# Direct preparation of the first weight jobs, on-chip shifted copies, another tile order in the first pair of blocks, and a zero-product start on TensorE

## The chip, the cores and the metric

The kernel runs on one core of a Trainium2 chip. The metric is the device time of one execution in microseconds (us), lower is better. The engines are named as the profile names them: PE is the matrix engine TensorE, PEld its weight loads, DVE the vector engine, ACT the scalar engine, POOL is GpSimd, SP the sync engine, which here does nothing but issue transfers (DMAs); SPq is its queue.

## What is computed

```python
# attention-like part: causal convolution, 7 taps per head, taps softmaxed
w = exp(weight - max(weight)); w = w / (sum(w) + 1e-9)
out[b, s, h, :] = sum over k of w[h, k] * x_pad[b, s + k, h, :]     # x: 2 x 4096 x 192
x = out.reshape(8192, 192)
# first layer
x = (sigmoid(x @ w_gate) * (x @ w_val)) @ w_out                     # 192 -> 1536 -> 192
# second layer
h = x @ w_in
g = where(h > 0, h, exp(min(h, 0)) - 1)
out = g @ w_out2                                                    # 192 -> 2048 -> 192
```

The activations are float32, the five weight matrices of the two layers are float64.

## The kernel before

**Tiling.** The 8192 tokens are 16 blocks of `TB` = 512. Blocks are taken in `GROUPS`: 0 to 2, 3 to 5, then pairs. Within a group, first all tiles of the first layer (kind 1, 12 tiles of 128 hidden units per block), then those of the second (kind 2, 16 tiles, two to a step). The list `steps` holds them; in the first group blocks 0 and 1 are interleaved tile by tile (`todo[:2]`), and block 2 follows alone. So steps 0 to 23 are kind 1 of blocks 0 and 1, steps 24 to 35 kind 1 of block 2, and step 36 begins kind 2 of blocks 0 and 1.

**Precision.** Each float32 factor is held as a high and a low part (float32r), and three products high x high, low x high and high x low are summed. 192 rows are 128 + 64; the matmuls work on 64 rows each, in pairs on the two halves of the array (`HALVES`). An activation block therefore has three parts: `n` (first 128 rows), `s` (the same with its halves exchanged, made by the DMAs of `exchange`, L144) and `r` (last 64 rows, doubled by the DMAs at L196).

**A step.** `front` (L280) makes the hidden tile of a step: 18 matmuls, 9 pairs, into two banks of the pool `ps_w`, which has four. `ew1` (L294) is ACT's sigmoid (L297) and DVE's product `g` (L299); that product frees the banks. For kind 2 `ew2` (L302) runs relu and exp on ACT (L309, L310) and `g` on DVE (L313), for each of the two banks. `split_hi` (ACT, L320) and `split_lo` (DVE, L326) make `gh` and `gl`, and `back` (L329) multiplies them with the output weights, `LAG` = 2 steps later; for two interleaved blocks one `back` takes both, 20 matmuls per tile. Since a front needs two of four banks, front k + 2 cannot finish its first products before the `g` of step k.

**Weights.** 34 jobs, `prep_in` (L252) and `prep_out` (L259), turn float64 into high and low float32r. `fetch` (L203) reads the tile from DRAM twice: `s` as it is, `m` shifted by two bytes, so that the bits below the high part lie in one 32-bit word. Then `narrow` (L219) runs ACT's absolute value (L232) and five DVE passes over 128x384 (L234, L236, L240, L242, L245), and `low` (L249) is a sixth. A job's parts are pieces of a generator; the table `PREPARED` says how many pieces are done by which step, and `CONV` says at which step the pieces of a block's convolution run. Both are due times written by hand: the program is recorded in that order, and each engine runs its instructions strictly in order.

**The start.** L447 to L460: transfers of the taps, x and the first three jobs are issued on SP; POOL makes an identity, ACT scales it by the taps (L131), and PE convolves the r part of blocks 0 and 1 and the n part of block 1 with these diagonals (L169, 14 float32 products, each two PE instructions); DVE convolves the n part of block 0 (L178, L176). L185 and L188 split the results.

**The change of layer.** At steps 36 and 37 the results of block 2's first layer are copied out of the accumulators by `sums` (L355: `one`, `two`). `early` (L514) lets `ew2` put these two copies between the two halves of a step.

Of the kernel before, what the change touches and what calls it, by code (L numbers as in the profile page):

```python
# [8 lines left out]
F32 = mybir.dt.float32  # L9
# [17 lines left out]
LAG = 2  # L27

# [7 lines left out]
    (-13.5, 0), (-11.5, 6), (-10.5, 9), (-9.5, 9), (-8, 12), (-7, 17), (-5.5, 17), (-1, 20), (21.5, 118),  # L36
# [5 lines left out]
    (0, 1): [-19, -10.5, -10, -10],  # L42
    (1, 0): [-18, -6.5, -6],
    (2, 0): [8.5 + k for k in range(7)] + [16.5, 17.5],
    (2, 1): [2.5 + k for k in range(6)] + [14.5, 18.5, 19.5, 20.5, 53.5, 54.5, 55.5],
# [11 lines left out]
def conv_glu_elu_kernel(  # L57
# [81 lines left out]
    def parts(kind, b, c):  # L139
        t = [xsp.tile([P, TB], F32R, tag=f"{c}{x}", name=f"x{c}{x}") for x in "hl"]  # L140
        parts_t.setdefault((kind, b), {})[c] = t
        return t

    def exchange(kind, b):  # L144

        for t, n in zip(parts(kind, b, "s"), parts_t[kind, b]["n"]):
            nc.sync.dma_start(f32(t[DR:]), f32(n[0:DR]))  # L147
            nc.sync.dma_start(f32(t[0:DR]), f32(n[DR:]))  # L148

    def load_x(b, i):  # L150
# [5 lines left out]
        else:  # L156
            for h in range(2):
                bi, t0 = divmod((b + h) * TB, S)
                nc.sync.dma_start(t[DR * h:DR * (h + 1)], xp[P:D, bi, t0:t0 + TB + PAD])
        yield  # L160

    def conv(b, i):
# [18 lines left out]
        for blocks in ([0], [1]) if i and b == 2 else ([0, 1], ) if i else ([0], ):  # L181
# [10 lines left out]
            if i:  # L192
                for n, ts, r in zip(blocks, made, rows):
                    other = slice(DR * (1 - n), DR * (2 - n))
                    for t in ts:
                        nc.sync.dma_start(f32(t[other]), f32(t[r]))  # L196
# [6 lines left out]
    def fetch(s, src, shift):  # L203

        n = P * 4 - shift
        src, s = src.bitcast(I16), s.bitcast(I16)
        if len(src.shape) == 3:
            m = D * 4 - shift
            d = s.rearrange("p (k m) -> p k m", k=src.shape[0])
            nc.sync.dma_start(d[:, :, 0:m], src.rearrange("k p m -> p k m")[:, :, shift:shift + m])  # L210
            return

        for i in range(2):
            d = s[DR * i:DR * (i + 1), 0:P * 8].rearrange("p (c m) -> p c m", c=2)
            e = src[:, P * 4 * i:P * 4 * (i + 1)].rearrange("(c p) m -> p c m", c=2)
            nc.sync.dma_start(d[:, :, 0:n], e[:, :, shift:shift + n])  # L216
        nc.sync.dma_start(s[:, P * 8:P * 8 + n], src[:, P * 8 + shift:P * 8 + shift + n])  # L217

    def narrow(src):  # L219
# [356 lines left out]
```

## Time and profile before

| | us |
|---|---|
| median of 3 runs | 1242.89 |
| lowest and highest run | 1242.01, 1244.04 |
| the profiled execution, its own time | 1242.56 |
| its span, first to last instruction | 1240.7 |
| what lies around the span | 1.86 |

Of the span PE is busy for 98%, PEld for 87%, DVE for 70%, ACT for 64%. The profile cuts the span in 40 slices: PE is at nine tenths or more in all but the first and the last, while DVE is at eight or nine tenths in slices 2 to 7 (31 to 217 us) and at five to eight afterwards. The DMA engines are busiest in the first six slices. A row of the timeline gives start, duration, engine, line, operation, out<-in, and in square brackets the idle time before it and what ended that. The "busy" of a matmul is modelled and overlaps its neighbours, so that pace is read from the starts.

### The profile page before, as it was taken

What the parts mean: (1) busy time and instruction counts of PE and PEld (TensorE: products, weight loads), DVE (VectorE), ACT (ScalarE), POOL (GpSimd) and SP (SyncE); (2) the same over time, 40 slices, a digit from 0 to 9 for tenths busy, and PEclk for the clock granted to TensorE, in tenths of its full rate; (3) what the DMA queues carried; (4) which work ended last, traced back from release to release, by engine and by line L of the source; (5) the groups of instructions that cost most, each with busy time, mean ns of one, the idle gap of its engine ahead of it and who ended that gap; (6) DMA issues with size and microseconds to landing.
All of it is one profiled execution on the core that took longest, in us unless ns stands there. A gap on an engine that the chain in (4) does not pass through costs nothing.

```text
span 1240.7 us, 25326 instructions
## 1 busy us (share of the span) xinstructions
PE 1215.8 (98%) x10268; PEld 1085.1 (87%) x10268; DVE 864.5 (70%) x1370; ACT 792.4 (64%) x1406; POOL 79.7 (6%) x63
## 2 busy tenths in 40 slices
PE   5999999999999999999999999999999999999997
PEld 2888789888889999999999889997888889998785
DVE  6898899785457876477665776666766667665564
ACT  4455688864348886348854498545884468744785
POOL 0000010100011000011000010010100100001100
PEclk9999999999999999999999999999999999999999
DMA  7756541311011020111111111020110211111100
GB/s 202 203 165 186 155 123 40 86 41 41 15 27 44 18 60 14 31 35 43 32 31 34 28 44 38 23 60 2 43 44 27 52 25 26 37 36 27 26 18 18
DMA packets 48965, 68.28 MB, mean 55 GB/s; under 512 B 6864, under 2 KB 29392, under 8 KB 48848
## 3 DMA queue, kind: packets, MB, share of 16 engines
q1 hardware_dynamic: 48848, 66.67, 20.4%
q8 instruction: 80, 1.31, 0.5%
q14 instruction: 37, 0.30, 0.1%
HBM read 33.09 MB, written 6.29 MB: 32 GB/s over the span
## 4 chain that ended last, share of the span: by engine, by line
PE 89%; DVE 3%; DMA 3%; SPq 2%; ACT 2%; issue 1%; DVEq 0%; ACTq 0%
PE ps L278 49%; PE a L278 40%; DMA s<-in_w_dram 2%; SPq L216 1%; DVE gl L326 1%; DVE g L299 1%; DMA m<-in_w_dram 0%; DVE xcv L176 0%; DVE r L245 0%; ACT e L310 0%; ACT e L309 0%; SPq L217 0%; ACT t L232 0%; SPq L148 0%; SPq L147 0%
## 5 line engine op out<-in xcount | busy, mean ns | idle before, releaser
L320 ACT CAST gh<-g 128x512 fp32r<-128x512 f32 x448 | 272.8, 618 | 181.5 <-DVE g L299 141.4
L326 DVE TENSOR_TENSOR gl<-g,gh 128x512 fp32r<-128x512 f32 x448 | 336.0, 764 | 75.3 <-ACT gh L320 64.7
L278 PE MATMUL a<-gh,w4s 64*128 64x512 f32 x1536 | 295.7, 392 | 0.1
L313 DVE SCALAR_TENSOR_TENSOR g<-e,ps 128x512 f32<-128x512 f32 x256 | 174.2, 686 | 117.9 <-ACT e L310 116.0
L278 PE MATMUL a<-gh,w2s 64*128 64x512 f32 x1152 | 251.8, 391 | 0.0
L278 PE MATMUL a<-gl,w4s 64*128 64x512 f32 x1024 | 244.2, 392 | 0.4 <-DVE gl L326 0.4
L299 DVE TENSOR_TENSOR g<-e,ps 128x512 f32<-128x512 f32 x192 | 131.5, 685 | 151.9 <-ACT e L297 146.8
L297 ACT ACTIVATE e<-ps 128x512 f32<-128x512 f32 x192 | 114.5, 596 | 179.1 <-PE ps L278 178.1
L278 PEld LDWEIGHTS a<-gh,w4s 64*128 64x128 f32 x1536 | 197.4, 185 | 17.0 <-DVE one L367 1.5
L278 PE MATMUL a<-gl,w2s 64*128 64x512 f32 x768 | 205.1, 392 | 1.5 <-DVE gl L326 1.5
L278 PEld LDWEIGHTS a<-gh,w2s 64*128 64x128 f32 x1152 | 163.0, 185 | 14.8 <-ACT gh L320 0.3
L309 ACT ACTIVATE e<-ps 128x512 f32<-128x512 f32 x256 | 150.5, 588 | 28.6 <-PE ps L278 28.0
L310 ACT ACTIVATE e<-e 128x512 f32<-128x512 f32 x256 | 161.9, 633 | 8.1
L278 PE MATMUL ps<-xsh,w1h 64*128 64x512 f32 x384 | 151.8, 395 | 5.6 <-DMA xsh<-xnh 5.3
L278 PEld LDWEIGHTS a<-gl,w4s 64*128 64x128 f32 x1024 | 145.1, 184 | 10.4 <-DVE gl L326 0.8
L278 PE MATMUL ps<-xsh,w1l 64*128 64x512 f32 x384 | 151.2, 394 | 0.0
L278 PE MATMUL ps<-xsl,w1h 64*128 64x512 f32 x384 | 150.6, 392 | 0.0
L278 PE MATMUL ps<-xnh,w1l 64*128 64x512 f32 x384 | 145.0, 393 | 0.0
L278 PE MATMUL ps<-xnh,w1h 64*128 64x512 f32 x384 | 144.7, 392 | 0.0
L278 PE MATMUL ps<-xnl,w1h 64*128 64x512 f32 x384 | 144.4, 392 | 0.0
L278 PEld LDWEIGHTS a<-gl,w2s 64*128 64x128 f32 x768 | 114.6, 184 | 12.7 <-DVE gl L326 3.3
L278 PE MATMUL ps<-xrh,w1h 64*128 64x512 f32 x384 | 120.2, 393 | 2.1 <-DMA xrh<-xrh 2.1
(92 smaller groups left out, 2565.2 us busy)
## 6 DMA issues: line engine op xcount, KB each, us to landing
xsh<-xnh SPq DMA_DIRECT2D x64, 128.0 KB, 2.3
xsl<-xnl SPq DMA_DIRECT2D x64, 128.0 KB, 2.3
s<-in_w_dram SPq DMA_DIRECT2D x60, 128.0 KB, 3.1
m<-in_w_dram SPq DMA_DIRECT2D x60, 127.8 KB, 3.0
three<-two SPq DMA_DIRECT2D x48, 128.0 KB, 2.2
s<-in_w_dram SPq DMA_DIRECT2D x14, 384.0 KB, 3.4
m<-in_w_dram SPq DMA_DIRECT2D x14, 383.5 KB, 3.9
x<-in_xp_dram SPq DMA_DIRECT2D x16, 259.0 KB, 3.2
```

The costliest lines, as they stand in the source:

```text
L216: nc.sync.dma_start(d[:, :, 0:n], e[:, :, shift:shift + n])
L278: return nc.tensor.matmul(ps, w, x, start=first, stop=last)
L297: nc.scalar.activation(s, gate, AF.Sigmoid)
L299: nc.vector.tensor_mul(g, s, val)
L309: nc.scalar.activation(e, h, AF.Relu, scale=-1.0)
L310: nc.scalar.activation(e, e, AF.Exp, scale=-1.0)
L313: nc.vector.scalar_tensor_tensor(g, e, -1.0, h, ALU.add, ALU.max)
L320: nc.scalar.copy(gh, g)
L326: nc.vector.tensor_sub(gl, g, f32(gh))
```

## The change

1. **Weights.** `m` is no longer read from DRAM. The first six jobs (`DIRECT`) have no `m`: their fifth pass takes nine bits of the high word and 15 of the low one, in two DVE instructions instead of one (24 bits instead of 25). The other 28 jobs make `m` by a DMA from `s` on the chip. `s` has four buffers instead of three, `m` two; jobs are fetched four ahead.
2. **Parts of x.** High and low parts lie in one tile, so that `exchange` is two DMAs instead of four, and the doubling of `r` one instead of two.
3. **Order of a front.** Both halves take part `n` first, then `s`, then `r`; the weights' chunk is chosen by `n ^ i`. Before, one half began with `n` and the other with `s`.
4. **Order of the steps.** Blocks 0 and 1 begin 0, 0, 1, 1 and go on 0, 1, 0, 1; the first back stands behind the fifth front.
5. **Start.** The two transfers of block 0's r part are issued on ACT's queue. PE begins with three float32 products of a tile of zeros.
6. **Change of layer.** The copies of block 2 no longer stand between the halves of a step, and the back of step 34 stands before the front of step 37.
7. `PREPARED` and `CONV` have other due times: 14 pieces before the first step instead of 20; block 2's convolution four steps later.

```diff
@@
-    (-13.5, 0), (-11.5, 6), (-10.5, 9), (-9.5, 9), (-8, 12), (-7, 17), (-5.5, 17), (-1, 20), (21.5, 118),
+    (-14.5, 0), (-13.5, 3), (-12, 3), (-11.5, 6), (-10, 6), (-8, 12), (-6.5, 12), (-1, 14), (18.5, 101), (21.5, 114),
...
-    (2, 0): [8.5 + k for k in range(7)] + [16.5, 17.5],
+    (2, 0): [12.5 + k for k in range(7)] + [20.5, 21.5],
...
     def exchange(kind, b):
-        for t, n in zip(parts(kind, b, "s"), parts_t[kind, b]["n"]):
-            nc.sync.dma_start(f32(t[DR:]), f32(n[0:DR]))
-            nc.sync.dma_start(f32(t[0:DR]), f32(n[DR:]))
+        parts(kind, b, "s")
+        n, s = (f32(parts_t[kind, b][c]) for c in "ns")
+        nc.sync.dma_start(s[DR:], n[0:DR])
+        nc.sync.dma_start(s[0:DR], n[DR:])
...
-                nc.sync.dma_start(t[DR * h:DR * (h + 1)], xp[P:D, bi, t0:t0 + TB + PAD])
+                (nc.sync if b else nc.scalar).dma_start(t[DR * h:DR * (h + 1)], xp[P:D, bi, t0:t0 + TB + PAD])
...
-    def narrow(src):
+    def narrow(src, copied):
...
-        s = stage.tile([P, n], I64, tag="s", name="s", bufs=3)
-        m = stage.tile([P, n], I64, tag="m", name="m", bufs=3)
-        fetch(s, src, 0)
-        fetch(m, src, 1)
...
+        s = stage.tile([P, n], I64, tag="s", name="s", bufs=4)
+        fetch(s, src)
+        words = s.bitcast(I32).rearrange("p (n two) -> p n two", two=2)
+        high = words[:, :, 1]
+        yield
+        if copied:
+            m = stage.tile([P, n], I64, tag="m", name="m", bufs=2)
+            nc.sync.dma_start(m.bitcast(I16)[:, 0:4 * n - 1], s.bitcast(I16)[:, 1:])
...
-        nc.vector.tensor_scalar(r, mid, 0x1FFFFFF, None, ALU.bitwise_and)
...
+        if copied:
+            nc.vector.tensor_scalar(r, mid, 0x1FFFFFF, None, ALU.bitwise_and)
+        else:
+            nc.vector.tensor_scalar(r, high, 0x1FF, 15, ALU.bitwise_and, ALU.logical_shift_left)
+            nc.vector.scalar_tensor_tensor(r, words[:, :, 0], 17, r, ALU.logical_shift_right, ALU.bitwise_or)
...
-        held = [[x[c] for c in "nsr"], [x[c] for c in "snr"]]
-        for c in range(3):
-            for k in range(3):
+        for n, part in enumerate("nsr"):
+            xh, xl = x[part][:, 0], x[part][:, 1]
+            for k, (wt, xt) in enumerate(((h, xh), (l, xh), (h, xl))):
                 for i, rows in enumerate(HALVES):
-                    xh, xl = held[i][c]
-                    wt, xt = ((h, xh), (l, xh), (h, xl))[k]
-                    mm(ps[i], wt[rows, c], xt[rows], c + k == 0, c + k == 4)
+                    mm(ps[i], wt[rows, n ^ i if n < 2 else n], xt[rows], n + k == 0, n + k == 4)
...
+                turns = [x for pair in zip(*todo[:2]) for x in pair]
+                if kind == 1:
+                    turns[1:3] = turns[2:0:-1]
+                todo[:2] = [turns]
...
+        warm = ew.tile([P, TB], F32, tag="g", name="warm", bufs=4)
+        nc.vector.memset(warm, 0.0)
+        ps = ps_w.tile([P, TB], F32, tag="w", name="ps")
+        for k in range(3):
+            nc.tensor.matmul(ps, warm[:, 0:P], warm, start=True, stop=True)
...
-            early = [end for k, _, end in ends if now and k < kind]
+            early = [end for k, _, end in ends if now and now[1] > 1 and k < kind]
```

The program's order on the engines shows what this moves. First PE from the start of the program, before; the numbers tell tiles apart: `ps_278` and `ps_279` are the two banks of step 0, block 0's parts are `xnh_186` and `xsh_196`, block 1's `xnh_254` and `xsh_258`.

```order
L169 MATMUL ps_162<-x1_102,gh_140 128x512 x4
L169 MATMUL ps_162<-x1_102,gl_141 128x512 x3
L169 MATMUL ps_171<-x0_113,gh_150 128x512 x4
L169 MATMUL ps_171<-x0_113,gl_151 128x512 x3
L278 MATMUL ps_278<-xnh_186,w1h_85 128x512
L278 MATMUL ps_279<-xsh_196,w1h_85 128x512
...
L278 MATMUL ps_278<-xrl_217,w1h_85 128x512
L278 MATMUL ps_279<-xrl_217,w1h_85 128x512
L278 MATMUL ps_319<-xnh_254,w1h_85 128x512
L278 MATMUL ps_320<-xsh_258,w1h_85 128x512
```

The same place in the changed program, where block 0's parts are `xn_191`, `xs_194` and `xr_203`:

```order
L466 MATMUL ps_122<-warm_120 128x512 x3
L171 MATMUL ps_160<-x1_102,gh_138 128x512 x4
L171 MATMUL ps_160<-x1_102,gl_139 128x512 x3
L171 MATMUL ps_169<-x0_109,gh_148 128x512 x4
L171 MATMUL ps_169<-x0_109,gl_149 128x512 x3
L280 MATMUL ps_242<-xn_191,w1h_85 128x512
L280 MATMUL ps_243<-xn_191,w1h_85 128x512
...
L280 MATMUL ps_242<-xs_194,w1h_85 128x512
L280 MATMUL ps_243<-xs_194,w1h_85 128x512
...
L280 MATMUL ps_280<-xn_191,w1h_85 128x512
L280 MATMUL ps_281<-xn_191,w1h_85 128x512
```

The zero products stand first, a front begins with six matmuls that need no exchanged part, and the second front is block 0's again. Second place, DVE from the end of block 0's convolution through the first weight job, before (`t_183`, `h_190`, `r_202` belong to that job):

```order
L176 SCALAR_TENSOR_TENSOR xcv_159<-x0_100,cwn_95,xcv_159 128x512 x6
L234 TENSOR_SCALAR t_183<-t_183 128x384
L236 TENSOR_SCALAR t_183<-t_183 128x384
L240 SCALAR_TENSOR_TENSOR h_190<-s_105,t_183 128x384
L242 TENSOR_SCALAR t_183<-h_190 128x384
L188 TENSOR_TENSOR xnl_187<-xcv_159,xnh_186 128x512
L245 TENSOR_SCALAR r_202<-m_106 128x384
L250 SCALAR_TENSOR_TENSOR w1l_86<-r_202,t_183 128x384
```

and in the changed program (`t_180`, `h_187`, `r_198`):

```order
L178 SCALAR_TENSOR_TENSOR xcv_157<-x0_100,cwn_95,xcv_157 128x512 x5
L231 TENSOR_SCALAR t_180<-t_180 128x384
L178 SCALAR_TENSOR_TENSOR xcv_157<-x0_100,cwn_95,xcv_157 128x512
L233 TENSOR_SCALAR t_180<-t_180 128x384
L237 SCALAR_TENSOR_TENSOR h_187<-s_105,t_180 128x384
L190 TENSOR_TENSOR xn_191<-xcv_157,xn_191 128x512
L239 TENSOR_SCALAR t_180<-h_187 128x384
L245 TENSOR_SCALAR r_198<-s_105 128x384
L246 SCALAR_TENSOR_TENSOR r_198<-s_105,r_198 128x384
L251 SCALAR_TENSOR_TENSOR w1l_86<-r_198,t_180 128x384
L190 TENSOR_TENSOR xr_203<-ps_160,xr_203 64x512
```

The first pass of the job now stands before the convolution's last tap, and L246 is the added pass. Third place, ACT at steps 36 and 37, before (`ps_2182` and `ps_2183` are the banks of step 37):

```order
L309 ACTIVATE e_2235<-ps_2182 128x512
L310 ACTIVATE e_2235<-e_2235 128x512
L366 COPY one_2240<-a2_1673 128x512
L366 COPY two_2241<-a3_1674 128x512
L309 ACTIVATE e_2246<-ps_2183 128x512
L310 ACTIVATE e_2246<-e_2246 128x512
```

and in the changed program (`ps_2128` and `ps_2129` are step 37's):

```order
L309 ACTIVATE e_2173<-ps_2128 128x512
L310 ACTIVATE e_2173<-e_2173 128x512
L309 ACTIVATE e_2178<-ps_2129 128x512
L310 ACTIVATE e_2178<-e_2178 128x512
L366 COPY one_2183<-a2_1612 128x512
L366 COPY two_2184<-a3_1613 128x512
```

The two copies moved behind the second half.

## Rows read from the trace of the kernel before

**Rows 1.** The page, part 1: busy time, share of the span, instructions.
```profile
PE 1215.8 (98%) x10268; PEld 1085.1 (87%) x10268; DVE 864.5 (70%) x1370; ACT 792.4 (64%) x1406; POOL 79.7 (6%) x63
```

**Rows 2.** Stretches: length, busy time (instructions), granted clock, DMA share, GB/s; PE, last DVE.
```profile
20.00:25.00 5.00, 2.53 (x19) 1.00 0.70 191
25.00:30.00 5.00, 0.01 (x2) 0.63 0.73 208
30.00:35.00 5.00, 5.00 (x30) 0.69 0.96 276
155.00:160.00 5.00, 3.45 (x27) 0.94 0.07 16
160.00:165.00 5.00, 5.00 (x35) 0.71 0.63 145
400.00:800.00 400.00, 400.00 (x3433) 1.00 0.14 34
...
40.00:100.00 60.00, 58.89 (x129) 1.00 0.59 174
```

**Rows 3.** Timeline of PE from 5 to 45 us.
```profile
5.55 5.51 PE L169 MATMUL ps<-x,gh 128*128 128x512 f32 x8 [5.55 <-DMA x<-in_xp_dram]
10.89 2.74 PE L169 MATMUL ps<-x,gl 128*128 128x512 f32 x6
19.57 0.49 PE L278 MATMUL ps<-xnh,w1h 64*128 64x512 f32 x1
23.58 0.50 PE L278 MATMUL ps<-xrh,w1h 64*128 64x512 f32 x1 [2.12 <-DMA xrh<-xrh]
29.98 0.76 PE L278 MATMUL ps<-xsh,w1h 64*128 64x512 f32 x1 [5.33 <-DMA xsh<-xnh]
44.48 0.76 PE L278 MATMUL a<-gh,w2s 64*128 64x512 f32 x4
```

**Rows 4.** Timeline of ACT and SP to 28 us; last a row of DMA issues.
```profile
9.65 0.54 ACT L232 ACTIVATE t<-s 128x384 f32<-128x384 f32 x1
20.96 0.50 SPq L196 DMA_DIRECT2D xrh<-xrh  x1
27.49 0.50 SPq L147 DMA_DIRECT2D xsh<-xnh  x1
...
m<-in_w_dram SPq DMA_DIRECT2D x3, 383.5 KB, 5.6
```

**Rows 5.** Timeline of DVE: a low part of a job, and one whole step.
```profile
12.87 0.56 DVE L250 SCALAR_TENSOR_TENSOR w1l<-r,t 128x384 fp32r<-128x384 int32 x1
...
61.02 0.68 DVE L326 TENSOR_TENSOR gl<-g,gh 128x512 fp32r<-128x512 f32 x1
61.62 0.68 DVE L299 TENSOR_TENSOR g<-e,ps 128x512 f32<-128x512 f32 x1
62.22 0.35 DVE L234 TENSOR_SCALAR t<-t 128x384 f32<-128x384 f32 x1
62.49 0.74 DVE L176 SCALAR_TENSOR_TENSOR xcv<-x,cwn,xcv 128x512 f32<-128x512 f32 x1
63.15 0.35 DVE L236 TENSOR_SCALAR t<-t 128x384 int32<-128x384 int32 x1
63.53 0.56 DVE L240 SCALAR_TENSOR_TENSOR h<-s,t 128x384 int32<-128x384 int32 x1
64.13 0.36 DVE L242 TENSOR_SCALAR t<-h 128x384 int32<-128x384 int32 x1
64.40 0.68 DVE L326 TENSOR_TENSOR gl<-g,gh 128x512 fp32r<-128x512 f32 x1
```

**Rows 6.** Timeline of PE and ACT where the layers change.
```profile
159.35 0.74 PE L278 MATMUL ps<-xsh,w3h 64*128 64x512 f32 x1 [1.55 <-DVE g L313]
162.87 0.85 PE L278 MATMUL a<-gh,w4s 64*128 64x512 f32 x4
...
156.36 0.57 ACT L366 COPY one<-a 128x512 f32<-128x512 f32 x1
157.30 0.61 ACT L309 ACTIVATE e<-ps 128x512 f32<-128x512 f32 x1
```

More of the change, by code (lines that the diff above doesn't have):

```diff
@@ L192, in conv, with fetch @@
             if i:
[L193 to L196, printed above, removed]
+                for n, r in zip(blocks, rows):
+                    t = f32(parts_t[1, b + n]["r"])
+                    nc.sync.dma_start(t[DR * (1 - n):DR * (2 - n)], t[r])
                 yield
-    def fetch(s, src, shift):
-        n = P * 4 - shift
-        src, s = src.bitcast(I16), s.bitcast(I16)
+    def fetch(s, src):
@@ L217, in fetch @@
-        nc.sync.dma_start(s[:, P * 8:P * 8 + n], src[:, P * 8 + shift:P * 8 + shift + n])
-    def narrow(src):
-        n = 3 * P
-        s = stage.tile([P, n], I64, tag="s", name="s", bufs=3)
-        m = stage.tile([P, n], I64, tag="m", name="m", bufs=3)
-        fetch(s, src, 0)
-        fetch(m, src, 1)
-        high = s.bitcast(I32).rearrange("p (n two) -> p n two", two=2)[:, :, 1]
-        mid = m.bitcast(I32).rearrange("p (n two) -> p n two", two=2)[:, :, 0]
+        for i, rows in enumerate(HALVES):
+            d = s[rows, 0:2 * P].rearrange("p (c m) -> p c m", c=2)
+            nc.sync.dma_start(d, src[:, P * i:P * (i + 1)].rearrange("(c p) m -> p c m", c=2))
@@ L265, in prep_out @@
             nc.scalar.copy(d[:, :, c, m], h[:, :, k])
[L266 removed]
+            low(d[:, :, o, q], r[:, :, k], unit, t[:, :, k])
             yield
@@ L443, in weights @@
                     yield n
-                if n + 3 < len(jobs):
-                    next(jobs[n + 3])
+                if n + 4 < len(jobs):
+                    next(jobs[n + 4])
         nc.sync.dma_start(cws, cw)
@@ L490, in conv_glu_elu_kernel @@
             now = steps[i] if 0 <= i < len(steps) else None
-            past = [i - LAG]
-            if now and now[1] < 2:
-                past = [i - LAG - 1, i - LAG] if now[1] else []
-            elif i >= LAG and i - LAG < len(steps) and steps[i - LAG][1] < 2:
-                past = [i - LAG - 1, i - LAG] if steps[i - LAG][1] else []
-            past = [steps[k] + (held.pop(k), ) for k in past if 0 <= k < len(steps)]
-            if past and past[0][1] == 0:
-                past = [past]
-            else:
-                past = [[x] for x in past]
+            past = [steps[k] for k in [i - LAG] if 0 <= k < len(steps)]
+            if past and past[0][1] < 2:
+                kind, b, j = past[0]
+                past = [(kind, n, j) for n in range(2)] if b else []
             if now:
@@ L505, in conv_glu_elu_kernel @@
             ends = []
-            for turns in past:
-                k, _, j, _ = turns[0]
-                ends += back(k, range(j, j + k), [(b, gs) for _, b, _, gs in turns])
+            if past:
+                kind_k, _, j_k = past[0]
+                ends = back(kind_k, range(j_k, j_k + kind_k), [(x[1], held.pop(index[x])) for x in past])
             his = split_hi(held.get(i - 1, []))
```

49 lines of the change are left out of this document (23 added, 26 removed).

## The prediction

> **What bounds the kernel now.** I read the page first, then stretches, then the timeline where the stretches are odd. PE is busy for 98% of the span [rows 1], so that time can only come from its gaps and its slow stretches. In 400 to 800 us it does 3433 matmuls without a gap [rows 2]: 0.1165 us each, 0.233 us a pair, so a front of 9 pairs takes 2.1 us and a back of two tiles (10 pairs) 2.33 us. The first 45 us are different: 2.53 us of work in 20 to 25, nothing in 25 to 30, then a granted clock of 0.69, a mean of the levels 1.2 and 2.4 GHz [rows 2]. The timeline says why [rows 3]. Step 0 starts at 19.57 when the convolutions end; at 23.58 it has waited 2.12 us for the doubled `r`, whose DMA SP issued only at 20.96 because weight transfers stood before it [rows 4]; step 1 belongs to block 1, and its first pair needs the exchanged part, issued at 27.49 [rows 4], so PE stands 5.33 us until 29.98 [rows 3] and comes back at half clock. The sixth front ends at 44.48, where a back begins [rows 3]. The second limit is DVE, 58.89 of 60 us in 40 to 100 [rows 2]. The second gap lies where the layers change: PE waits until 159.35 for a `g` of DVE and then runs one front in 3.52 us, to 162.87 [rows 6], at a clock of 0.71 [rows 2].
>
> **Part A, the start.** All edits at the start go together, because one chain results.
>
> PE. A float32 product is two PE passes. In the first row eight passes take 5.51 us; later six take 2.74, at starts 0.43 apart [rows 3]: the clock's two levels. 28 passes at the upper one are 12.0 us, and from 5.55 to 19.57 they took 14.0: the slow beginning cost 2.0 us. The zeros are six passes. PE can begin when DVE has filled a 128x512 tile; no row has this, so I bound it by an idle engine's start and DVE's 128x512 passes (0.74 us at most [rows 5]), which gives 0.8 to 1.6, and take 1.4. The zeros end at 4.0 if all are fast and at 6.5 if all are slow; if they take over just the 2.0 us that the convolutions lost, at 1.4 + 6 x 0.43 + 2.0 = 6.0, later than x arrives. I take that; the convolutions end at 6.0 + 12.0 = 18.0 instead of 19.57. Behind them, in order, stands step 0, whose `s` and `r` are no longer behind `m`: 1.2 MB of `m` for three jobs leave the queue before them, so I give it no wait.
>
> The x transfers on ACT's queue put two issues before ACT's other work: 0.5 to 0.6 us each by SP's rows [rows 4], of which I take 0.4 us as delay after overlap with the wait for the taps. ACT's first pass of job 0, done at 10.2 before [rows 4], is then done at 10.6. The Trainium skill, DMA: Bandwidth & Descriptors, section Issuing engines are not separate DMA queues, holds that issuing from a second engine saves issue time only, as all queues share the transfer engines. By that x would come 1.2 us earlier at best, and nothing in the sum changes, since x is not the last to arrive.
>
> DVE. From 10.6 on it has no hole and becomes the chain. Its pitch I read from starts in a full step [rows 5]: `gl` and `g` 0.60 each, a tap 0.66, a pass on 128x384 0.27 before an independent instruction and 0.38 before a dependent one, a two-input pass (L240) 0.60 before a dependent one and 0.47 before another; L250 lasts as long as L240. The added pass L246 is not in the trace: at least 0.27 (a one-input pass), at most 0.74 (a tap); I take L240's 0.60, the same kind and size. A direct job is then 0.38 + 0.38 + 0.60 + 0.27 + 0.38 + 0.60 + 0.47 = 3.1 us. Ahead of the end of the third `g` (step 2) the order puts four direct jobs (12.5 with the fourth's halved last pass), two passes of a fifth (0.7), one tap (0.7), four splits of x (2.4) and three `g` and two `gl`, the last `g` counted to its end (3.1): 19.4 us, so it ends at 30.0. Before it fronts 0 to 3 all fit: they wait on banks, not on weights. Front 4 needs that bank and ends at 32.1. The first back needs the `gl` of step 2, which DVE reaches after the rest of the fifth job and one tap (2.6 us), and which takes 0.7: 33.3; two of its ten pairs run ahead, the other eight end at 35.2. Front 5 ends at 37.3. Before: 44.48. **A = -7.2 us.**
>
> From there PE needs 6.5 us for two fronts and a back, and DVE about as much: the order lists 61 us of durations for steps 4 to 19 in either program. Both engines have the lead, so it is kept. In steps 15 to 22 the changed order lists 28.5 us of durations for DVE against 25.9, some 2 us more after overlap, which PE's 26 us there should cover. Cost 0; without that cover, up to +2.
>
> The on-chip `m` is issued on SP behind the fetch of a later job, and by the order its pass on DVE comes two steps later, some 6.5 us. DMAs of `m` landed in 5.6 us (median) in the crowded first 45 us [rows 4], so I cost it at nothing. Fewer DMAs of `exchange` and `r` in the steady stretch gain nothing, for PE waits for none of them in 400 to 800 us [rows 2].
>
> **Part B, the change of layer.** ACT puts `one` and `two`, 157.30 - 156.36 = 0.94 us, before the relu of step 37's second half [rows 6], and its `g` releases PE at 159.35. Moved behind, the same `g` comes 0.94 us earlier. PE's wait of about 2.0 us halves, and a wait of 1 us should leave the clock up, which gives back 3.52 - 2.1 = 1.4. The copies now delay `gh` and `gl` of step 37 instead, and the back that needs them: I take 0.4. **B = -1.9 us**; bounds: 0 if the back takes the wait over, -2.4 if it does not.
>
> **Sum.** 1242.56 (the profiled execution, 1240.7 span and 1.86 around it) - 7.2 - 1.9 = 1233.5. That execution is 0.33 below the median of the runs, so I forecast **1233.8** (-0.73%).
>
> **Rivals.**
>
> *PE cold in the bank waits.* In 22 to 33 us PE now waits for `g` three or four times, 0.6 to 1.5 us each. If that lowers the clock, a front costs 3.5 instead of 2.1, as the cold one did; DVE hides it for two fronts, and front 4 and front 5 show it: +2.8, 1236.6. Against it: with half of 20 to 25 idle the clock stayed at 1.00 [rows 2]. The Trainium skill, TensorE: Matmul & The Clock Gate, section A second HAM failure mode, says that idling between groups of matmuls while cycling through PSUM banks makes the clock swing; by it this rival would hold. The row of 20 to 25 does not show that, the row of 155 to 160 is nearer to it. Chance 0.15.
>
> *Zeros do not lift the clock.* Then the six passes end at 6.5 and the convolutions take their 14.0 us after them, ending at 20.5; the split of block 1's `n` moves DVE by 2.2: 1236.0. Nothing in the trace has such products. Chance 0.12.
>
> *Slower: the copies come late.* SP issues in order, and each copy stands behind a fetch that waits for a free `s`. If a copy lands more than 6.5 us after its issue, DVE waits in each of the 28 copied jobs, most of them where DVE is full. The gain is gone at 9.1 / 28 = 0.33 us a job; at 0.45 us it is 1246.4. For it: a chain of two transfers where two independent ones were. Against it: 1.2 MB less of traffic in the start, and 5.6 us was a median under the worst load. Chance 0.06.
>
> *The lead is lost on the way.* DVE's extra passes are not covered (+2), step 26's chain or a late part of block 2 stops PE as well, and B is 0: 1238 to 1241. Chance 0.15.
>
> The forecast itself has 0.52; its own range is 1231 to 1235.5.
>
> **How the numbers follow.** About 0.2% (2.5 us) is what a measurement of this kernel can tell from no change. Low end: B at -2.4 and L246 at 0.27 (six times 0.33) give 1231.3, and some of DVE's dependent pitches may overlap better; 1230. High end: the first two rivals and most of the lost lead, 1239.5. Faster by over 0.2% (below 1240.4): the forecast, both first rivals and about half of the lost lead, 0.87. Same: the rest of the lost lead and a copy that is a little late, 0.08. Slower: 0.05.
>
> **What would show it.** Right: PE's first convolution pass near 6 us and step 0 near 18; no DMA among PE's longest waits in the first 45 us, but DVE's `g` (L299) for the fronts of steps 2 to 4; the third `g` near 29 and the sixth front's end near 37; no wait of DVE for `m`; the gap before step 39 about 1 us, with the clock up. Wrong: a clock below 1 between 20 and 35 us, passes of 0.86 us after the zeros, DVE idle on DMA at L243, or a back that waits for `gl` by more than a microsecond at the change of layer.

## The result and the profile after

The changed kernel takes 1232.5 us (median of 4 runs, 1232.05 to 1233.98) against 1243.47 (4 runs of the kernel before beside it): a ratio of 0.9915, 95% interval 0.9898 to 0.9932. Five later runs gave 1232.67, ratio 0.9932 (0.9918 to 0.9946). The profiled execution took 1232.05 us, 10.51 less than the one of before; its span is 1230.2.

PE is busy for 99% of the span (98% in [rows 1]). The stretches that answer to [rows 2] (length, busy time and instructions, granted clock, DMA share, GB/s; the last row is DVE, the others PE; the DMA share counts the packets that start in a stretch, so it can pass 1):

```profile
20.00:25.00 5.00, 4.25 (x36) 1.00 0.84 216
25.00:30.00 5.00, 3.88 (x31) 1.00 0.66 162
30.00:35.00 5.00, 4.58 (x37) 1.00 0.50 152
150.00:155.00 5.00, 3.15 (x25) 1.00 0.30 70
...
40.00:100.00 60.00, 58.88 (x130) 1.00 0.54 173
```

TensorE's two bad stretches are gone: 20 to 30 us holds 67 instructions instead of 21, at full clock, and the change of layer, now at 150 to 155 us, stays at 1.00 too. DVE is as full in 40 to 100 as before. PE's waits show what is left; each row is who waited for whom, us in total, times, longest:

```profile
PE a L280 <- DVE gl L326: 2.9, 4, 1.3
PE ps L280 <- DVE g L299: 1.8, 2, 1.0
...
```

The two rows left out are the start's wait for the tile of zeros (1.5) and a `g` at the change of layer (0.6); no DMA is among them. The timeline of PE in the start answers to [rows 3]:

```profile
1.48 4.94 PE L466 MATMUL ps<-warm 128*128 128x512 f32 x6 [1.48 <-DVE warm L462]
6.26 3.60 PE L171 MATMUL ps<-x,gh 128*128 128x512 f32 x8
18.37 0.50 PE L280 MATMUL ps<-xn,w1h 64*128 64x512 f32 x2
23.81 0.49 PE L280 MATMUL ps<-xn,w1h 64*128 64x512 f32 x1 [0.75 <-DVE g L299]
30.05 0.49 PE L280 MATMUL ps<-xn,w1h 64*128 64x512 f32 x1 [1.03 <-DVE g L299]
32.03 0.84 PE L280 MATMUL a<-gh,w2s 64*128 64x512 f32 x4
33.25 0.50 PE L280 MATMUL a<-gl,w2s 64*128 64x512 f32 x1 [0.37 <-DVE gl L326]
37.16 0.76 PE L280 MATMUL a<-gh,w2s 64*128 64x512 f32 x4
```

The zeros run from 1.48 us; the first eight convolution passes then take 3.60 us where they took 5.51. Step 0 starts at 18.37. The fronts of steps 2 and 4 wait for `g`, the first back for `gl`, and the sixth front ends at 37.16 where a back begins, as at 44.48 before. DVE and SP over the same time ([rows 4, 5]):

```profile
10.56 0.36 DVE L231 TENSOR_SCALAR t<-t 128x384 f32<-128x384 f32 x1 [0.78 <-ACT t L229]
...
13.62 0.56 DVE L246 SCALAR_TENSOR_TENSOR r<-s,r 128x384 int32<-128x384 int32 x1
14.22 0.56 DVE L251 SCALAR_TENSOR_TENSOR w1l<-r,t 128x384 fp32r<-128x384 int32 x1
...
29.32 0.68 DVE L299 TENSOR_TENSOR g<-e,ps 128x512 f32<-128x512 f32 x1
```
```profile
15.39 1.22 SPq L197 DMA_DIRECT2D xr<-xr  x2
...
20.62 0.60 SPq L150 DMA_DIRECT2D xs<-xn  x1
```

From 10.56 on no DVE row of this trace carries a wait until past 37 us; the added pass L246 takes 0.60 from its start to the next; the third `g` ends at 30.00. SP issues the doubled `r` at 15.39 instead of 20.96, and block 1's exchange at 20.07 and 20.62 instead of 27.49. Last the change of layer, which answers to [rows 6]:

```profile
150.82 0.49 PE L280 MATMUL ps<-xn,w3h 64*128 64x512 f32 x1 [0.57 <-DVE g L313]
152.79 0.85 PE L280 MATMUL a<-gh,w4s 64*128 64x512 f32 x4
154.93 0.50 PE L280 MATMUL a<-gl,w4s 64*128 64x512 f32 x1 [1.28 <-DVE gl L326]
```
```profile
150.68 0.68 DVE L367 TENSOR_TENSOR one<-a,one 128x512 f32<-128x512 f32 x1
151.28 0.68 DVE L367 TENSOR_TENSOR two<-a,two 128x512 f32<-128x512 f32 x1
...
152.15 1.47 DVE L243 TENSOR_SCALAR r<-m 128x384 int32<-128x384 int32 x1
...
154.19 1.29 DVE L326 TENSOR_TENSOR gl<-g,gh 128x512 fp32r<-128x512 f32 x2
```

The front behind the wait takes 1.97 us (150.82 to 152.79) instead of 3.52. But the back then waits 1.28 us for `gl`, a wait that the trace of before does not have. Ahead of that `gl` DVE now has the two additions that belong to the copies (L367); before, they stood ahead of the `g` that releases TensorE.

**Where the time came from.** Three marks are in every trace: the sixth front's end, the first front of the second layer, and, as the first mark behind the change of layer, the copy `one` (L364 on ACT) with which the first block leaves the second layer, called the second `one`. The last two, before and after:

```profile
148.59 0.39 PE L278 MATMUL ps<-xnh,w3h 64*128 64x512 f32 x1
231.56 0.57 ACT L364 COPY one<-a 128x512 f32<-128x512 f32 x1
```
```profile
141.03 0.40 PE L280 MATMUL ps<-xn,w3h 64*128 64x512 f32 x2
222.92 0.57 ACT L364 COPY one<-a 128x512 f32<-128x512 f32 x1
```

Both kernels were traced once more in the experiments; the last column holds those two traces against each other.

| | before | after | gained so far | second pair of traces |
|---|---|---|---|---|
| sixth front ends | 44.48 | 37.16 | 7.32 | 44.27 - 37.19 = 7.08 |
| second layer's first front | 148.59 | 141.03 | 7.56 | 147.32 - 141.05 = 6.27 |
| second `one` | 231.56 | 222.92 | 8.64 | 229.65 - 223.07 = 6.58 |
| last `one` | 1232.17 | 1222.19 | 9.98 | 1231.43 - 1222.27 = 9.16 |
| span | 1240.7 | 1230.2 | 10.5 | 1240.0 - 1230.3 = 9.7 |

In the first pair the start gave 7.3, the first layer another 0.2, the change of layer 1.1. In the second pair the start gave 7.1, the first layer lost 0.8 of it, and the change of layer gave 0.3. The 1.3 us (in the second pair 2.6) between 231 and 1232 come where nothing was meant to change and TensorE hardly waits in either kernel. From the second to the last `one` it took 1000.61 us before, 999.27 after, and between 998.06 and 1001.78 in the twelve experiments. I count it as scatter, but this is not shown: the three longest of the fourteen stretches (1000.61, 1001.34, 1001.78) are those of the three traces in which the weights are read twice from DRAM. The last 0.5 is mostly the last transfer's latency.

### The profile page after: what moved, and what is told of

It is laid out like the page before. It is cut to its first block, busy times and chain, and to the rows that moved or that the text cites. A ratio compares the mean times of both kernels' runs of the same rounds, so it can differ in the third digit from the quotient of the medians.

```text
span 1230.2 us, 25137 instructions
## 1 busy us (share of the span) xinstructions
PE 1215.4 (99%) x10274; PEld 1101.7 (90%) x10274; DVE 868.7 (71%) x1377; ACT 793.1 (64%) x1406; POOL 80.2 (7%) x63
## 4 chain that ended last, share of the span: by engine, by line
PE 89%; DVE 5%; ACT 2%; DMA 1%; issue 1%; SPq 0%; ACTq 0%; DVEq 0%
PE ps L280 50%; PE a L280 40%; DMA s<-in_w_dram 1%; DVE g L299 1%; DVE gl L326 1%; DVE h L237 0%; DVE r L243 0%; ACT e L310 0%; ACT e L309 0%; DVE xcv L178 0%; ACT gh L320 0%; DMA x<-in_xp_dram 0%; DVE t L233 0%; DVE g L313 0%; DVE t L239 0%
## 5 line engine op out<-in xcount | busy, mean ns | idle before, releaser
L280 PE MATMUL a<-gh,w2s 64*128 64x512 f32 x1152 | 238.0, 393 | 0.1
L280 PE MATMUL ps<-xn,w1h 64*128 64x512 f32 x768 | 191.9, 392 | 2.0 <-DVE g L299 1.8
L280 PE MATMUL a<-gl,w2s 64*128 64x512 f32 x768 | 191.4, 393 | 1.3 <-DVE gl L326 1.3
L280 PE MATMUL ps<-xs,w1h 64*128 64x512 f32 x768 | 190.2, 392 | 0.0
L280 PE MATMUL ps<-xr,w1h 64*128 64x512 f32 x768 | 189.9, 390 | 0.0
L280 PEld LDWEIGHTS a<-gl,w4s 64*128 64x128 f32 x1024 | 132.0, 185 | 11.6 <-DVE gl L326 2.5
L280 PEld LDWEIGHTS ps<-xn,w1h 64*128 64x128 f32 x768 | 107.9, 184 | 12.1 <-DVE g L299 4.1
L280 PE MATMUL ps<-xn,w3h 64*128 64x512 f32 x512 | 118.0, 392 | 0.6 <-DVE g L313 0.6
L280 PE MATMUL ps<-xr,w3h 64*128 64x512 f32 x512 | 117.7, 391 | 0.0
L280 PE MATMUL ps<-xs,w3h 64*128 64x512 f32 x512 | 117.5, 391 | 0.0
```

The costliest lines, as they stand in the source:

```text
L280: return nc.tensor.matmul(ps, w, x, start=first, stop=last)
```

## The experiments

Single times scatter by some 2 us here, and the median of the kernel before by 3 from one set of runs to the next, so parts of a few microseconds are read from the marks of one trace each. The changed kernel returns to them closely: its second trace had its second layer at 141.05 and its second `one` at 223.07. The kernel before does so less: its second layer came at 148.59 and at 147.32. A part of less than about 1 us is therefore shown only where several traces agree on it.

**The changed kernel again.**

> The changed kernel once more, as the yardstick for the runs beside it: 1231.5 to 1233.5 us by either theory. In its trace the places of its first look should return within 0.5 us (step 0 near 18.4, the sixth front's end near 37.2, the first front of the second layer near 141).

Measured: 1232.67 us; step 0 at 18.66, the sixth front's end at 37.19, the second layer at 141.05. As expected; this is the yardstick below.

**Without the zeros.**

```diff
-        warm = ew.tile([P, TB], F32, tag="g", name="warm", bufs=4)
-        nc.vector.memset(warm, 0.0)
-        ps = ps_w.tile([P, TB], F32, tag="w", name="ps")
-        for k in range(3):
-            nc.tensor.matmul(ps, warm[:, 0:P], warm, start=True, stop=True)
```

> The changed kernel without the zero products and their tile. In the changed kernel TensorE's real convolutions start at 6.26 us and end at 18.37; DVE, which has no idle time from 10.56 us on, splits their last result at 19.36 without waiting. Theory (DVE's chain is the bound of the start): without zeros the convolutions start near 5.4, lose the 2.0 us of slow passes and end near 19.5, so DVE waits only some 0.3 to 0.5 us at that split and the end moves by as much: 1232.8 to 1233.2 against the changed kernel's 1232.5. Rival (the zeros carry the start, as the prediction priced it): the end moves by about 2 us, to 1234.5.

Measured: 1234.83 us, ratio 0.9944 (0.9931 to 0.9956). Step 0 at 20.86, second layer at 143.38: 2.33 us later than the yardstick. The theory fell and the rival held. The timelines of PE and DVE in this run:

```profile
6.18 6.17 PE L171 MATMUL ps<-x,gh 128*128 128x512 f32 x8 [6.18 <-DMA x<-in_xp_dram]
```
```profile
16.17 1.41 DVE L190 TENSOR_TENSOR xr<-ps,xr 64x512 fp32r<-64x512 f32 x2 [1.41 <-ACT xr L187]
21.59 0.69 DVE L190 TENSOR_TENSOR xn<-ps,xn 128x512 fp32r<-128x512 f32 x1 [0.77 <-ACT xn L187]
```

The first eight passes take 6.17 us, and DVE waits 1.41 and 0.77 us for two results of the convolutions, 2.18 together. So DVE is not the only chain: in the changed kernel the convolutions' last result is ready 0.3 us before DVE takes it (ACT's copy ends at 19.07, DVE's split starts at 19.36; in the second trace 19.36 and 19.39), and the zeros are what keeps them below DVE.

**The old order of steps.**

```diff
-                if kind == 1:
-                    turns[1:3] = turns[2:0:-1]
```

> The changed kernel with the steps of blocks 0 and 1 in the order 0, 1, 0, 1 from the first on; the first back then stands behind the fourth front. Theory (DVE's chain is the bound): the second front needs block 1's exchanged part, issued at 20.62 us and landed near 23, so TensorE waits some 2 us there instead of at the banks; the work of DVE up to the third g is the same, and the end moves by less than 1 us either way: 1231.5 to 1233.5. Rival (the order of the steps took away the wait of 5.33 us before): 2 to 5 us slower, 1234.5 to 1237.5.

Measured: 1235.98 us, ratio 0.995 (0.9937 to 0.9962); second layer at 144.27, 3.2 later, 2.7 if the later step 0 (19.18) is taken off. The rival held. PE's wait, and its stretches:

```profile
25.19 0.79 PE L280 MATMUL ps<-xs,w1h 64*128 64x512 f32 x2 [2.95 <-DMA xs<-xn]
```
```profile
20.00:25.00 5.00, 2.24 (x20) 0.94 0.72 171
25.00:30.00 5.00, 4.81 (x22) 0.50 0.65 169
```

The expected wait was short of the measured one (2 against 2.95), and what follows was not expected at all: the clock falls to 0.50 and 22 instructions fill 25 to 30, and DVE then waits 2.61 us for the sigmoid of that front.

**Both old orders.** The edit above, and

```diff
...
-                    mm(ps[i], wt[rows, n ^ i if n < 2 else n], xt[rows], n + k == 0, n + k == 4)
+                    part = x[("nsr", "snr")[i][n]]
+                    wt, xt = ((h, part[:, 0]), (l, part[:, 0]), (h, part[:, 1]))[k]
+                    mm(ps[i], wt[rows, n], xt[rows], n + k == 0, n + k == 4)
```

> As the run before, and each front takes its parts as before the change: one half of the array begins with the n part, the other with the exchanged one. Theory (DVE's chain is the bound): the second front waits for the exchanged part at its first pair, near 23.2 us instead of 20.6, and ends near 25.4; the third and fourth end near 27.5 and 29.6, and as DVE's g and gl release the rest, the end moves by 0 to 1.5 us: 1232.5 to 1234. Rival (the two orders together are the gain of the start): 5 us or more slower, 1237.5 or later.

Measured: 1237.0 us, ratio 0.9958 (0.9945 to 0.9972); second layer at 143.30, 2.25 later. Neither theory nor rival: the wait for the exchanged part is 2.39 us at 23.47, the clock in 25 to 30 is 0.86, and by the marks the loss is no larger than with the old order of steps alone (2.25 against 3.2). But the traced execution took 1235.03 us, the fastest of the five; by the medians the loss is 4.3 us, just short of the rival and 1.0 larger than with the old steps alone. So by the marks the order of the steps is worth 2 to 3 us in the changed kernel; whether the order inside a front adds to it stays open.

**Copies between the halves again (part B undone).**

```diff
-            early = [end for k, _, end in ends if now and now[1] > 1 and k < kind]
+            early = [end for k, _, end in ends if now and k < kind]
```

> The changed kernel with block 2's two copies between the halves of step 37 again, all else as changed. Theory (part B as predicted, reduced by the wait of 1.28 us that the back has for gl in the changed kernel): the g that releases TensorE comes 0.9 us later, the wait grows from 1.0 to 1.9 us, the granted clock falls and the next front takes 3.5 instead of 2.1 us, and the wait for gl shrinks by 0.9 to 1.3: 1.0 to 1.4 us slower, 1233.5 to 1233.9. Rival (the back takes the whole wait over, so the place of the copies is worth nothing): 1232.3 to 1232.7. Rival (the back's wait is a new one and would have come anyway): 2.3 us slower, 1234.8.

Measured: 1233.29 us, ratio 0.993 (0.9917 to 0.9942). From the second layer's first front to the second `one` it takes 82.35 us against 82.02 in the yardstick and 81.89 to 82.03 in the six other traces with the changed order there: the place of the copies is worth 0.3 us. Nearest is the rival by which the back takes the wait over. PE there:

```profile
152.30 0.49 PE L280 MATMUL ps<-xn,w3h 64*128 64x512 f32 x1 [1.54 <-DVE g L313]
```
```profile
150.00:155.00 5.00, 3.46 (x27) 1.00 0.34 79
```

The wait is that of before (1.54; 1.55 in [rows 6]), yet the clock stays at 1.00 and the wait of 1.28 us for `gl` is gone. This put the prediction's 1.4 us for the clock in doubt.

**The kernel before again.**

> The kernel before once more, for its trace. At the change of layer TensorE stood 2.04 us between two starts (157.31 to 159.35) and the granted clock then fell to 0.50; in the changed kernel with the copies back between the halves it stood 2.04 us too (150.26 to 152.30) and the clock stayed at 1.00. Theory (a gap of this length is at the edge, and the fall is chance): the gap returns at 2.0 us, the clock may hold or fall, and the time from the second layer's first front to the second copy of the accumulators is 81.9 to 82.4 us if it holds and 83.0 if it falls. Rival (something in the kernel before makes it fall each time): 83.0 again. Time 1241 to 1243.

Measured: 1241.77 us, ratio 1.0009 (1.0 to 1.0018).

```profile
158.08 0.49 PE L278 MATMUL ps<-xsh,w3h 64*128 64x512 f32 x1 [1.54 <-DVE g L313]
160.04 0.85 PE L278 MATMUL a<-gh,w4s 64*128 64x512 f32 x4
```
```profile
155.00:160.00 5.00, 3.46 (x28) 1.00 0.29 66
```

The same program with the same wait holds its clock this time: the front takes 1.96 us, not 3.52, and the stretch between the marks 82.33, not 82.97. The fall that the prediction charged to the kernel before does not come in every execution. From this trace to the changed kernel's first: TensorE's gap shrinks from 2.04 to 1.07 us from start to start, the front behind it stays (1.96 and 1.97), and the back grows from 5.11 to 6.30, by as much as DVE's two additions take (1.20), which stood ahead of the `g` and now stand ahead of the `gl`. What remains is one later gap of 0.8 us that is gone.

The start of this trace is not that of the first one either: TensorE waits 2.56 us for the doubled `r` and 3.34 for the exchanged part (2.12 and 5.33 in [rows 3]), the clock is at 0.50 from 23.8 to 34.0, and the sixth front ends at 44.27, 0.2 earlier.

**Weights from DRAM again (part 1 undone).** `fetch`, `narrow`, `low`, `prep_in` and `prep_out` as before the change, and

```diff
-            next(jobs[3])
...
-                if n + 4 < len(jobs):
-                    next(jobs[n + 4])
+                if n + 3 < len(jobs):
+                    next(jobs[n + 3])
```

> The changed kernel with the weights read as before the change: m comes from DRAM for all 34 jobs, three buffers each for s and m, jobs fetched three ahead; orders, zeros and due times as changed. Theory (the weight transfers ahead of the doubled r and of the exchange in SP's queue made TensorE's waits of 2.12 and 5.33 us): SP issues the r doubling and the exchanges some 4 to 7 us later than at 15.39 and 20.62, TensorE waits for DMAs in the first three fronts and runs cold after it, while DVE saves 0.6 us on each of the first jobs: 2 to 5 us slower, 1234.5 to 1237.5. Rival (orders and zeros are the whole gain, the way of the weights is neutral): 1231.5 to 1233.

Measured: 1235.83 us, ratio 0.9957 (0.9944 to 0.997); second layer at 144.14, 3.1 later. The size is the theory's, the place is not: SP issues the `r` doubling at 15.81 and block 1's exchange at 20.33 and 20.84, within half a microsecond of the changed kernel (block 0's is 1.2 late, at 14.28, and nothing waits for it). What comes late are the weights themselves: the fourth job's `s` is issued at 17.08 instead of 8.23 and the fifth's from 21.48 on instead of 16.67, behind the transfers of `m` and with three buffers instead of four. ACT in this run:

```profile
22.61 0.55 ACT L233 ACTIVATE t<-s 128x384 f32<-128x384 f32 x1 [3.03 <-DMA s<-in_w_dram]
...
23.47 0.58 ACT L296 ACTIVATE e<-ps 128x512 f32<-128x512 f32 x1
...
28.11 0.55 ACT L233 ACTIVATE t<-s 128x384 f32<-128x384 f32 x1 [2.68 <-DMA s<-in_w_dram]
```

ACT waits 3.03 and 2.68 us for the fourth and fifth job, with the sigmoids of steps 0 and 1 behind it in its order (23.47 and 28.55); DVE waits 1.27 and 2.15 us for these, and TensorE for the banks. In the changed kernel ACT waits for no transfer between 10 and 45 us. The DMA engines are fuller as well. PE's stretches, and the exchanges of the first 45 us (KB each, median us to landing), first of this run, then of the changed kernel:

```profile
20.00:25.00 5.00, 4.21 (x33) 1.00 1.05 268
25.00:30.00 5.00, 3.99 (x20) 0.73 1.12 261
```
```profile
xs<-xn SPq DMA_DIRECT2D x4, 256.0 KB, 4.7
```
```profile
xs<-xn SPq DMA_DIRECT2D x4, 256.0 KB, 3.5
```

With the DMA engines' share at 1.05 and 1.12 instead of 0.84 and 0.66, the exchange lands over a microsecond later. PE waits for ACT's sigmoid (0.56 us at 24.10) and for the exchange (0.80 us at 26.58), two short gaps close together, and the clock falls at 27.25. The run undoes several things at once (the source of `m`, the direct passes, the buffers, and how far ahead jobs are fetched), and no run parts them.

**All jobs direct.** `DIRECT = 34`.

> The changed kernel with all 34 jobs prepared directly, none copied: 28 added passes of 0.6 us on DVE, 17 us, from about 33 to 160 us, and no transfer of m at all. Theory (DVE is full from 10 us to about step 23: 58.88 of 60 us busy in 40 to 100): some 18 of the 28 fall before 110 us, 11 us, of which 1 to 2 lie in DVE's holes and 2 to 3 in jobs that are done ahead of need, and the rest stops TensorE: 5 to 8 us slower, 1237.5 to 1240.5. Rival (TensorE has the lead, and DVE's added passes are covered by jobs done ahead): 1232 to 1234.

Measured: 1243.41 us, ratio 1.0014 (1.0005 to 1.0023). Second layer at 149.44, 8.4 later; the change of layer 85.63 instead of 82.02, another 3.6. DVE being full is confirmed, and the expected size was low: it credited jobs that are done ahead of need, and left out that the second layer's jobs run at the change of layer too. The 3.6 hold a wait for `gl` of 1.88 us and a fall of the clock behind it. Of some 16.8 us of added passes (28 times 0.60) 10.7 by the medians, 12.0 by the marks, reach the end. So with direct passes for every job nothing is left of the gain; with `m` from DRAM (the run before this one) two thirds of it were left.

**Block 0's `r` part on SP again.** `nc.sync.dma_start` for both blocks.

> The changed kernel with block 0's r part of x issued on SP again. Theory (as the prediction priced it: 0.4 us of delay on ACT, paid by the first pass of the first job, while x is not the last to arrive because the zeros end later): DVE's chain begins 0.3 to 0.4 us earlier than at 10.56 but meets the convolutions' results at 19.36, so the sixth front ends between 0.4 us earlier and the same: 1232.0 to 1232.7. Rival (SP then issues the first weights 1.2 us later, and their job starts late): 0.5 to 1.2 us slower, 1233.1 to 1233.9.

Measured: 1232.99 us, ratio 0.994 (0.9927 to 0.9954). DVE, to be held against 10.56 above:

```profile
10.07 0.36 DVE L231 TENSOR_SCALAR t<-t 128x384 f32<-128x384 f32 x1 [1.39 <-ACT t L229]
```

The sixth front ends at 36.67 and the second layer starts at 140.48, 0.5 and 0.57 us earlier; the times of the runs can't tell so little. The two issues cost ACT 0.5 us. They bring nothing for it: issued from 0.73 on by ACT, block 0's `r` part landed at 5.58; issued from 1.63 on by SP, at 5.26. By the marks this part of the change is a small loss.

**Versions that go further.** Fewer pieces of weights before the first steps, and DVE's `gl` of step 37 ahead of the pieces:

```diff
-    ... (-6.5, 12), (-1, 14), (18.5, 101), ...
+    ... (-6.5, 12), (-0.5, 12), (2.5, 25), (18.5, 101), ...
@@
+            if his and now == (2, 0, 2):
+                held[i - 1], his = split_lo(held[i - 1], his), None
             run(i)
```

> The changed kernel with two moves. First, fewer pieces of weights stand before the first steps (12 instead of 14 before step 0, 25 instead of 29 by step 2.5, the same 101 by step 18.5), so that DVE reaches g of steps 0 to 2 some 1.4 to 1.9 us earlier. Second, at the first step of the second layer's third front DVE does gl before the weights' pieces and not behind them, against the wait of 1.28 us. Theory: TensorE's waits for g (0.75 and 1.03 us) and gl (1.28 us) go, 1 to 3 us faster, 1229.5 to 1231.5. Rival (DVE is full up to step 23, and what it puts off in the start it owes by step 18): only the second move shows, 1231.2 to 1232.

Measured: 1232.21 us, ratio 0.9923 (0.991 to 0.9936); second layer at 140.00 (1.05 earlier), second `one` at 221.37 (1.7 earlier). The time lies a little above the rival's range, and within what the runs scatter by. At the sixth front's end it was 2.2 ahead (34.97); over 1 us of that was lost by the second layer, as the rival said. PE's waits for `g` in the start are gone, and a wait of 1.52 us for block 1's exchange stands in their place. That exchange follows a split at 19.36 for which DVE waited for nothing (the convolutions' result was ready at 18.64), so DVE's order sets this wait too. Then that with `DIRECT = 3` and block 1's last piece a step later:

```diff
-                for n in (0.5, 1 if (k, b) == (2, NB - 1) else 2.5):
+                for n in (0.5, 1 if (k, b) == (2, NB - 1) else 3.5 if (k, b) == (1, 1) else 2.5):
```

> The version with fewer pieces of weights ahead of the first steps, with two more moves: only the first three jobs are direct, so that jobs 4 to 6 save DVE one pass of 0.6 us each; and the last part of block 1's first results (two DVE additions that wait for ACT) comes one step after block 0's, since TensorE stands 1.2 us at step 26 in every trace, where DVE does both ahead of a gl. Theory: the second layer starts 1.2 us earlier for the gap and up to 1.2 for the lead that was lost between 50 and 120 us, near 138 to 139 against 140.0 and 141.05, and the time is 1 to 2 us under that version's: 1230.2 to 1231.2. Rival (the copies of jobs 4 to 6 delay the exchange or land late, or the lead is lost to DVE all the same): 1232 to 1233.

Measured: 1229.85 us, ratio 0.9913 (0.99 to 0.9927) in a set where the kernel before took 1240.54. Second layer at 138.97, second `one` at 220.42: 2.65 us ahead of the yardstick. What the two added moves are worth singly was not tried. And with block 0's `r` part on SP:

> The last version with block 0's r part of x issued on SP again, as that move alone brought the second layer 0.57 us forward. Theory (ACT's two issues delay its table load and so the first weight job by 0.5 us): DVE's chain begins near 10.07 instead of 10.56, the second layer near 138.4 to 138.9, and the time is 0 to 1 us under the last version's 1229.85: 1228.9 to 1229.9. Rival (TensorE waits for the exchanged part of block 1 there, which the convolutions set, not ACT): no change beyond scatter, 1229.5 to 1230.5, with the second layer near 139.

Measured: 1229.95 us, ratio 0.9905 (0.9889 to 0.9922); DVE begins at 10.14, the second layer at 138.50, the second `one` at 219.88. By the marks it is 0.5 us better still, by the runs it equals the last one. Both beat the changed kernel, by 2.8 and 2.7 us in the medians and by 2.65 and 3.2 at the second `one`, though the intervals of their ratios to the kernel before overlap its own. The cleanest comparison is within one set: all four runs of the version before the last (1228.41 to 1231.10) lie below all five of the changed kernel with `r` on SP (1232.02 to 1234.28).

## Why the prediction was right, and where it was not

Forecast 1233.8 in 1230 to 1239.5; measured 1232.5 and 1232.67. The sum was made for the profiled execution, 1233.5, which took 1232.05.

**Part A.** Forecast -7.2, measured -7.32, and nearly each step came where it was put: DVE's chain from 10.6 (10.56), step 0 at 18.0 (18.37, in the second trace 18.66), the third `g` at 30.0 (30.00), the fifth front's end at 32.1 (32.03), `gl` at 33.3 (TensorE goes on at 33.25), the back's end at 35.2 (35.08), the sixth front's end at 37.3 (37.16). Pitches read from starts, added along DVE's order, were enough; L246 at the 0.60 of L240 was exact.

What the text did not see is how thin the cover is. It treated DVE as the chain and step 0 as lying beside it. The runs show two chains that end within 0.3 us of each other, and other inputs close behind, so that each part is needed: without the zeros 2.3 us go, with the old order of steps 2 to 3, with the weights from DRAM 3.1. How slowly the zeros run differs between executions: step 0 came between 17.85 and 19.31 in the eleven traces with zeros, and where it came after 19 DVE did wait at that split (0.59 us with the old order of steps). So the zeros took out most of the slow beginning, not all of it each time.

The reason given for TensorE's waits before, that `m` stood before `s` and `r` in the queue, is half of what the trace of before shows. In it ACT waits for weights too:

```profile
21.32 0.55 ACT L232 ACTIVATE t<-s 128x384 f32<-128x384 f32 x1 [3.16 <-DMA s<-in_w_dram]
21.89 0.58 ACT L185 CAST xnh<-ps 128x512 fp32r<-128x512 f32 x1
```

The convolutions end at 19.57, but the first step of block 1's split (L185) stands behind that wait. DVE ends the split at 23.20, where the changed kernel has it at 20.05 (1.2 of these 3.2 us are the later end of the convolutions); only then comes the queue, in which SP issues six weight transfers from 23.43 to 27.39 ahead of the exchange at 27.49. So weights that come late hold ACT, and the queue holds the exchange. With the weights from DRAM in the changed order the first of the two returns, with the sigmoids behind it, and the second does not. How much of the 5.33 us before each is worth stays open: the merged transfers (part 2) and the due times (part 7) were not tried by themselves.

The first layer was costed at 0, or up to +2 without cover. It measured -0.2 in the first pair of traces and +0.8 in the second, so whether the lead is kept whole is not shown.

**The rivals.** "PE cold in the bank waits" didn't come: the clock is 1.00 from 20 to 35 us with waits of 0.75, 1.03 and 0.37 us. The Trainium skill, TensorE: Matmul & The Clock Gate, section A second HAM failure mode, would have the clock swing there; the rows of 20 to 35 do not show it. "Zeros do not lift the clock" didn't come either; its price of 2.2 us was right, as the run without them shows 2.33. "The copies come late" didn't: no wait of DVE for `m` stands in the trace, and the copies land in 3.2 us (median) in the first 45. The slowest of the 28 took 6.2, not far below the 6.5 us that the rival allowed. "The lead is lost on the way" didn't come as a whole: B turned out near 0, which was one of its three conditions, and the first layer lost at most 0.8 of the 2 us. That such a loss is real, the run with direct passes for every job shows: 8.4 us by the second layer.

**ACT's queue.** Priced at 0.4 us, measured at 0.5. The bound of 1.2 us by which x could come earlier was far off: its last part came 0.3 later than with all issues on SP.

**Part B** is the step that failed inside a right total. Forecast -1.9 from -0.94 for the copies, -1.4 for the clock and +0.4 for the delayed back. Measured in the first pair of traces -1.1. The first two came as put: the wait halves, and the front takes 1.97 instead of 3.52. The third was mis-sized: TensorE waits 1.28 us for `gl`, one of the prediction's own signs of being wrong. The prediction moved ACT's copies and not the two additions of DVE that go with them (L367, 1.20 us); those now stand ahead of the `gl`. Behind them one DVE pass took 1.47 us (below), but that is not new; the kernel before has the like in both its traces (1.46 us), in the first:

```profile
159.21 1.46 DVE L242 TENSOR_SCALAR t<-h 128x384 int32<-128x384 int32 x1
```

And the 1.4 us were taken from one execution: the second trace of the kernel before holds its clock after the same wait. Against that trace the change of layer gives 82.33 - 82.02 = 0.3 us. The back takes the wait over, as the prediction's bound of 0 had it; the forecast's own range from 0 to -2.4 held what came, the reason for choosing the far end did not hold.

**The total** came 1.4 us lower in the profiled execution although B gave 0.8 less: the steady stretch was 1.3 shorter, the tail 0.5, the first layer 0.2. The prediction has no term for the steady stretch and the tail. In the second pair of traces the parts are 7.1 for the start, -0.8 for the first layer, 0.3 for B and 3.1 for the steady stretch and the tail together. So the closeness of the sum owes something to luck in B and in the steady stretch; the start does not.

## What to carry to other kernels

Where one engine is full, the start can be forecast to a few tenths by adding the starts of its rows along the new order; but then ask of each input how long it lies ready before it is taken, since 0.3 us of slack means that another chain is as long. Price a clock fall only after a second execution has shown it. When a pass is freed or a wait removed, what stands next in the same engine's order takes its place, as `gl` behind the weights' pieces did, and moving that (0.6 us in three traces) was worth more than the part that had been moved (0.3). What is prepared late holds the engine that prepares it, and with it the work that stands behind: look for waits on other engines, not only on the full one.

## What the runs showed of the hardware

**Gaps and the clock.** All gaps here are from one start of a matmul to the next. TensorE stood 2.04 us in three traces at the change of layer (the kernel before twice, and the changed one with the copies back): once the granted clock fell to 0.50 for 3.4 us, twice it stayed at 1.00. It also stayed after a gap of 1.90 (the version with fewer pieces) and after one of 2.52 (the kernel before, 21.06 to 23.58, where the stretch of 20 to 25 has 1.00). It fell in or just behind gaps of 2.27 (all jobs direct), 2.79 (both old orders), 2.96 (the kernel before, second trace), 3.34 (old steps) and 5.80 (the kernel before). Single gaps up to 1.70 left it at 1.00 everywhere, but it fell behind three of 0.94, 0.72 and 1.19, all between 23.16 and 26.58 us (weights from DRAM). So the length of a single gap does not decide by itself.

**DVE beside POOL.** The pass L243 takes 0.35 us. In the changed kernel's trace up to 240 us two of the 28 took 1.47 and 1.41 (at 152.15 and 161.30), those that ran beside one of POOL's 128x512 operations of 1.29 us:

```profile
152.10 1.29 POOL L379 TENSOR_TENSOR xn<-one,xn 128x512 fp32r<-128x512 f32 x1 [150.79 <-ACT xn L378]
```

The pass started at 152.15 and ended at 153.62, just behind it (153.39), at the moment when TensorE needed the `gl` behind it. In the second trace of the kernel before, L242 took 1.46 instead of 0.36 us beside such an operation, and a `gl` 1.78 instead of 0.69. The Trainium skill, SBUF — State Buffer, section SBUF: two separate sides, has GpSimd and certain kinds of DVE operation exclude each other on a port pair that the two engines share; these rows agree.

**Zeros.** Products of zeros lift the clock: their six passes took 4.38 to 5.49 us in the traces. In seven of the eleven traces the convolutions behind them ran at the upper level (0.43 to 0.47 us a pass) from the first on, in the other four from the second on, with a first pass of 0.72 to 0.85. In the three traces without zeros the first four to six convolution passes were slow.
